# A convolution-plus-MLP kernel on one core: spectra of two chunks at a time, and turns of Z done by transposing transfers

## The chip, the core and the metric

The kernel runs on one core of a Trainium2 chip. TensorE (PE) multiplies matrices into PSUM, and its weight loads (PEld) are shown as a row of their own; VectorE (DVE) and ScalarE (ACT) do the elementwise work and copy PSUM to SBUF; GpSimd (POOL) builds tables; SyncE (SP) issues nearly all transfers, in order, and 16 DMA engines carry them out. The metric is the device time of one execution in microseconds. A profiled execution gives a span (first to last instruction) and a time of its own, which is slightly longer than the span.

## The reference, cut to what matters

```python
# A: a diagonal state-space convolution over L = 2048 positions, D = 512 channels, N = 128 states
P = exp(dt*A[:, :, None] * l)                 # complex, l rounded to bf16
K = einsum("dn,dnl,dn->dl", Cc, P, dt*Bc).real
y = irfft(rfft(pad(u.T)) * rfft(pad(K)))[:, :L]        # causal convolution per channel
h = x + bf16(y).T + u * Dskip,   u = layernorm(x)
# B: an MLP on the result, F = 1376
h2 = h + gelu(layernorm(layernorm(h)) @ w1 + b1) @ w2 + b2
```

The 2048 positions are worked as two blocks of 1024 (block 0 and block 1; in a name of the change "A" and "B"). Block 0 of the output needs block 0 of u and block 0 of K. Block 1 needs u1 with K0 and u0 with K1, and what block 0 carries over.

## The kernel before, in words

One SBUF arena `ar` holds everything; a view is an address in it, and the same address is used by several views in turn. PSUM is four slots of 128x1024 f32. All work is handed to a small planner (`Sched`) as operations with an engine (or a choice of ACT and DVE), a cost, what they read and write, and a rank from the table `RANK`; it places them one after the other and the kernel emits them in that order. Each engine then runs its own list in order, and semaphores follow the true dependences. A "soft" dependence is one of the planner alone: it sets the order of the list and makes no semaphore.

The 512 channels are four chunks of 128 (`CW`, `NCH`). The stages, with the lines of the profile:

- **Setup.** Loads, layernorm statistics of x (L878), and the tables of sines: T, TP1 and TP2 (L605, three of 2048 columns), after int32 codes made on POOL (L584, L1302). T has three parts [cos, sin, cos] per frequency so that a slice of two neighbours gives X or its swapped twin Xs; DVE copies the third part (L582, 128x1024 bf16).
- **aexps** (L960 to L965) fills the powers EA with accumulating matmuls and exponentials, two PSUM slots in turn; L700 and L698 build its 17 scaled identities.
- **austage** (L900) multiplies normalised u by a small block matrix for both blocks and writes it to DRAM (AU_d), to come back with another partition order. This write and read is called a bounce.
- **chain** (L988 to L1014) makes the complex exponentials of K for two halves of the channels: matmuls, a Sin on ACT (L1003), products on DVE (L1013, L1014).
- **kgen** (L1035, L1036) forms K of one chunk with 256 small matmuls (33 columns and 20 output rows each); **kspec** (L1080) does a first transform stage of K for one block and one chunk and writes it to DRAM (AK_d); **kload** (L1096) loads it back and does the second stage, one 128x128 matmul per frequency.
- **xspec0** (L917) does the second stage of u for block 0 and all channels: per frequency two matmuls of 512 columns, [re, im] into X0 and the swapped [im, re] into X0s, 16 PSUM tiles of 1024 columns. **xspec** (L935) does block 1 chunk by chunk, 16 tiles as well, into two buffers XB used in turn.
- **inverse** multiplies spectra on DVE (L1114) and transforms back with TP1 and TP2 (L1123), 128 rows per matmul. Its result Z has to be turned (frequency group and position change places). For chunks 2 and 3 of block 0 (`TURN`) TensorE does it (L1138: 16 transposes, copied out by ACT or DVE). For the six others Z goes to DRAM (Z_d) and comes back in the new order.
- **tail** (L1208, L1213) adds x and the turned Z in PSUM, takes statistics (L1218), runs the short layernorm chain (L593, L598, L582, L584 on 128x4), normalises (L1232, L1234) and transposes with TensorE (L1239); there are four tails, two per block.
- **mlp** (L1257, L1259, L1274, L1276), four of them, and the output.

L536 and L538 are the one helper that copies PSUM to SBUF (`evac`) on ACT or DVE, and L548 the one that issues plain transfers. Products (`PR`), the normalised rows of the tail (`y2s`) and int32 codes share addresses, as do the spectra of block 0, the turned Z and the MLP weights.

Of the kernel before, what the change touches and what calls it, by code (L numbers as in the profile page):

```python
# [1404 lines left out]
```

## Time and profile before

| what | value |
|---|---|
| median of 3 runs | 301.11 us (300.15 to 301.65) |
| profiled execution, own time | 297.31 us |
| its span | 295.5 us |
| granted TensorE clock, mean | 0.971 |
| busy: PE, PEld | 232.2 us, 140.1 us |
| busy: ACT, DVE, POOL | 198.0 us, 185.5 us, 46.0 us |
| DMA moved | 34.15 MB, 43873 of 57191 packets under 512 B |

A busy time is the union of an engine's instructions; the matmuls are pipelined, so the mean duration of one (219 ns for L1123) is far above its share of the busy time. The page also has the span in slices, the chain of work that ended last, groups of instructions by line with what ended the idle time before them, and the transfers with their time from issue to landing.

### The profile page before, as it was taken

The page shows a single profiled execution, that of the slowest core. Times are in us where ns is not written, and L with a number is a line of the kernel's source. Part 1 is how long each engine was busy: PE and PEld are TensorE (multiplying, and loading weights), DVE is VectorE, ACT ScalarE, POOL GpSimd, SP SyncE. Part 2 cuts the span into 40 slices and gives each one's busy share as a digit, 9 for nine tenths or more (in the row PEclk, how much of TensorE's full clock was granted, in tenths as well). Part 3 has the DMA queues.
Part 4 walks back from the last instruction along what each step waited for, and adds up shares of the span by engine and source line. Part 5 has one row for each costly group of instructions (what it writes and reads, how often), then busy time and mean ns, then how long its engine had stood idle before and what let it go on. Part 6 is the DMA issues. An engine that isn't in the chain of part 4 may idle for free.

```text
span 295.5 us, 8030 instructions
## 1 busy us (share of the span) xinstructions
PE 232.2 (79%) x3337; PEld 140.1 (47%) x3360; DVE 185.5 (63%) x392; ACT 198.0 (67%) x257; POOL 46.0 (16%) x213
## 2 busy tenths in 40 slices
PE   6204948788997797499977629799999999898983
PEld 2101313344576546487855226578674334443431
DVE  3999999999986798035736784656850375311021
ACT  5988999999956994157984848685528338832700
POOL 9992102996000000000000000000000000000000
PEclk9999998999999999979999958999999999999999
DMA  7700113799101679997896300656564011002011
GB/s 145 265 0 2 35 41 91 195 231 341 35 4 57 192 167 241 239 235 257 249 219 155 71 1 0 176 141 201 144 159 110 0 46 29 1 18 57 0 35 36
DMA packets 57191, 34.15 MB, mean 116 GB/s; under 512 B 43873, under 2 KB 52034, under 8 KB 57154
## 3 DMA queue, kind: packets, MB, share of 16 engines
q1 hardware_dynamic: 55954, 33.24, 42.3%
q8 instruction: 26, 0.43, 0.6%
q10 hardware_dynamic: 1200, 0.39, 0.5%
q14 instruction: 11, 0.09, 0.1%
HBM read 19.47 MB, written 13.63 MB: 112 GB/s over the span
## 4 chain that ended last, share of the span: by engine, by line
PE 47%; DVE 22%; issue 10%; ACT 9%; DMA 5%; SPq 3%; POOL 2%; DVEq 0%; ACTq 0%; POOLq 0%
PE ps L1274 12%; PE ps L1257 9%; ACT ar L536 6%; PE ps L1123 5%; DVE ar L593 4%; PE ps L1036 3%; SPq L548 3%; PE ps L1035 3%; DVE ar L878 3%; DVE ar L598 3%; DVE ar L538 3%; PE ps L997 2%; PE ps L1080 2%; DMA ar<-AU_d 2%; DVE ar L1218 2%
## 5 line engine op out<-in xcount | busy, mean ns | idle before, releaser
L536 ACT CAST ar<-ps 128x1024 bf16<-128x1024 f32 (+3 forms) x91 | 75.2, 889 | 49.5 <-DVE ar L1218 9.8
L538 DVE CAST ar<-ps 128x1024 bf16<-128x1024 f32 (+2 forms) x33 | 38.8, 1194 | 19.0 <-PE ps L1096 12.8
L1257 PE MATMUL ps<-ar 128*128 128x512 bf16 (+1 forms) x170 | 40.6, 384 | 2.8 <-ACT ar L536 1.4
L1274 PE MATMUL ps<-ar 128*128 128x512 bf16 (+1 forms) x168 | 40.1, 379 | 3.1 <-DVE ar L1276 2.7
L1114 DVE TENSOR_TENSOR ar<-ar 128x1024 bf16<-128x1024 bf16 x48 | 30.1, 688 | 17.1 <-PE ps L1123 14.6
L1259 ACT ACTIVATE ar<-ps,ar 128x512 bf16<-128x512 f32 (+1 forms) x44 | 29.7, 689 | 14.5 <-PE ps L1257 14.1
L1003 ACT ACTIVATE ar<-ps 128x1024 bf16<-128x1024 int16 x36 | 35.5, 1042 | 3.5 <-PE ps L997 3.0
L584 POOL TENSOR_SCALAR ar<-ar 128x128 bf16<-128x128 bf16 (+5 forms) x40 | 30.5, 783 | 15.6 <-DMA ar<-ar 10.4
L1276 DVE TENSOR_TENSOR ar<-ps,ar 128x512 bf16<-128x512 f32 x16 | 11.0, 690 | 32.7 <-PE ps L1274 25.6
L1257 PEld LDWEIGHTS <-ar 128*128 128x128 bf16 (+1 forms) x176 | 17.6, 101 | 22.1 <-issue 4.3
L1274 PEld LDWEIGHTS <-ar 128*128 128x128 bf16 (+1 forms) x176 | 16.7, 97 | 22.8 <-issue 4.9
L1036 PE MATMUL ps<-ar 128*20 128x33 bf16 x512 | 20.0, 248 | 6.6 <-issue 6.6
L1218 DVE BATCH_NORM_STATS2 ar<-ps 128x6 f32<-128x512 f32 x16 | 11.1, 697 | 21.7 <-PE ps L1213 16.7
L1123 PE MATMUL ps<-ar 128*128 128x128 bf16 x384 | 24.1, 219 | 0.6 <-DVE ar L1114 0.3
L997 PE MATMUL ps<-ar 128*32 128x256 f16 x560 | 21.4, 275 | 3.8 <-ACT ar L1003 1.6
L1123 PEld LDWEIGHTS <-ar 128*128 128x128 bf16 x384 | 22.3, 98 | 3.3 <-DVE ar L1114 1.0
L1036 PEld LDWEIGHTS <-ar 128*20 128x20 bf16 x512 | 17.8, 125 | 8.2 <-issue 8.2
L997 PEld LDWEIGHTS <-ar 128*32 128x32 f16 x560 | 13.9, 97 | 12.6 <-issue 12.1
L1035 PE MATMUL ps<-ar 128*20 128x33 bf16 x512 | 19.7, 249 | 0.2
L1014 DVE TENSOR_TENSOR ar<-ar 128x1024 bf16<-128x1024 bf16 x26 | 17.8, 702 | 1.6 <-ACT ar L1003 1.5
L1013 DVE TENSOR_TENSOR ar<-ar 128x1024 bf16<-128x1024 bf16 x26 | 18.1, 709 | 0.9 <-ACT ar L1003 0.8
L1035 PEld LDWEIGHTS <-ar 128*20 128x20 bf16 x512 | 17.5, 124 | 0.5 <-issue 0.2
(92 smaller groups left out, 307.8 us busy)
## 6 DMA issues: line engine op xcount, KB each, us to landing
AU_d<-ar SPq DMA_DIRECT2D x16, 256.0 KB, 4.6
ar<-AU_d SPq DMA_DIRECT2D x8, 512.0 KB, 5.9
AK_d<-ar SPq DMA_DIRECT2D x16, 256.0 KB, 4.2
ar<-AK_d SPq DMA_DIRECT2D x8, 512.0 KB, 5.6
Z_d<-ar SPq DMA_DIRECT2D x12, 256.0 KB, 3.2
ar<-Z_d SPq DMA_DIRECT2D x6, 512.0 KB, 4.6
ar<-in_A_u_dram SPq DMA_DIRECT2D x4, 512.0 KB, 7.1
ar<-in_A_u_dram SPq DMA_DIRECT2D x16, 128.0 KB, 5.4
```

What stands on the lines that cost most here:

```text
L536: act.copy(out_fn(), in_fn())
L538: dve.tensor_copy(out_fn(), in_fn())
L584: en.tensor_scalar(a, b, f(s1), f(s2), op0, op1)
L997: pe.matmul(pst(p)[32 * g:32 * g + 32, 256 * j:256 * j + 256], lhsT=W2[DELTAS.index(d)].ap(), rhs=S2[g].ap()[:, ch0:ch0 + 256], start=Fals ...
L1003: add("ACT", c_act(1024), lambda e, p=p, sc=sc, cs=cs: act.activation(sc[cs].ap().rearrange("p a b -> p (a b)"), pst(p, i16).rearrange("p ...
L1035: pe.matmul(o, lhsT=Ar.ap()[:, :, d], rhs=Br.ap()[:, :, d], start=True, stop=False, tile_position=(0, 32 * g))
L1036: pe.matmul(o, lhsT=Ai.ap()[:, :, d], rhs=Bi.ap()[:, :, d], start=False, stop=True, tile_position=(0, 32 * g))
L1114: add("DVE", c_dve(1024, 2), lambda e, kf=kf, x=x, pr_=pr_, f0=f0: dve.tensor_tensor(pr_.ap(), kf[f0:f0 + 8].ap(), x[f0:f0 + 8].ap(), ALU. ...
L1123: pe.matmul(pst(p)[:, 128 * k:128 * k + 128], lhsT=a, rhs=b_, start=(n == 0), stop=(n == len(jobs) - 1))
L1257: pe.matmul(pst(p)[:fs, 512 * z:512 * z + 512], lhsT=w1s[dc].ap()[:, fc * P:fc * P + fs], rhs=ybuf.ap()[:, dc, :], start=(dc == 0), stop=( ...
L1259: add("ACT", c_act(512, 1), lambda e, p=p, z=z, fc=fc, fs=fs: act.activation(hT.ap()[:fs, fc, :], pst(p)[:fs, 512 * z:512 * z + 512], ACT. ...
L1274: pe.matmul(pst(p)[:, 512 * z:512 * z + 512], lhsT=hT.ap()[:fs, fc, 128 * t:128 * t + 128], rhs=w2s[fc].ap()[:fs], start=(fc == 0), stop=( ...
```

## The change

The parts of a spectrum (real and imaginary) are laid in the free dimension: two neighbouring frequencies share the 128 partitions, 64 each. One stage (`fstage`) now serves u and K. It uses 64-column weights in two column positions of the array, and its output holds each value once, so that the swapped twins X0s and Xs are gone; the product reads X with its two parts reversed. The inverse uses 64-row matmuls in two row positions, into two PSUM banks. K is staged for two chunks at a time (`kgen` still works by chunk): chunks 0 and 1 for both blocks in one bounce, chunks 2 and 3 in one bounce per block. All of block 1's K is staged ahead of the tails, and block 1's u is loaded and transformed in one go into a buffer of its own. Every turn of Z, and the transposes of three of the four tails, are transposing transfers from SBUF to SBUF on SP's queue, 128x2048 bf16 each; only the first tail keeps TensorE transposes. Products, Z, x rows and normalised rows have buffers per block, and the addresses of weights and spectra move with them. aexps takes turns in three PSUM slots and needs 19 scaled identities. The rank table is another one, with two constants of the planner's model.

```diff
-NZ = 3
-NKG = 3
-TURN = (2, 3)
+KB = [[(0, 1)], [(0,), (1,)]]
...
-    AK_d = [[dram.tile([16, P, CW], bf16, name=f"AK_d{b}{c}") for c in range(NCH)] for b in range(2)]
-    Z_d = [[dram.tile([P, 16, CW], bf16, name=f"Z_d{b}{c}") for c in range(NCH)] for b in range(2)]
+    AK_d = [[dram.tile([16, P, 2 * CW * len(bs)], bf16, name=f"AK_d{q}{n}") for n, bs in enumerate(KB[q])] for q in range(2)]
...
-    T = take(bf16, 16, 3, 64)
-    TP1 = take(bf16, 16, P)
-    TP2 = take(bf16, 16, P)
+    T = take(bf16, 16, 2, 64)
+    TP = [take(bf16, 8, P) for _ in range(3)]
...
+    def xspec(b, X, pr, soft=()):
         S.pr = pr
         for q in range(4):
...
+        fstage(X, 4, soft)
+    def fstage(v, nb, soft=()):
+        pr, w = S.pr, 128 * nb
+        nf = 8 // nb
+        for f0 in range(0, 16, nf):
             p = Ps()
             def fn(e, p=p, f0=f0):
+                for k in range(0, nf, 2):
                     for r in range(2):
+                        for h in range(2):
+                            f = f0 + k + h
+                            pe.matmul(pst(p)[64 * h:64 * h + 64, w * (k + r):w * (k + r) + w], lhsT=T.ap()[:, f, r, :], rhs=v.ap()[:, f, :], start=True, stop=True, tile_position=(0, 64 * h))
+            evac(lambda f0=f0: v[f0:f0 + nf].ap().rearrange("p a b -> p (a b)"), lambda p=p: pst(p), 1024, [p], [v[f0:f0 + nf]])
...
+    def kstage(q, ak, D, kf, bs, pr):
+        nb = len(bs)
+        for n, b in enumerate(bs):
+            kspec(b, q, pr + n, ak, nb, n)
+        for cp in range(2):
+            dma("SP", lambda cp=cp: D.rearrange("(k z) p d -> z p k d", z=2)[cp], lambda cp=cp: ak.ap()[:, 8 * cp:8 * cp + 8, :], 524288 * nb, ...)
+        for fh in range(2 * nb):
+            dma("SP", lambda fh=fh, n=n: kf[n * fh:n * fh + n].ap(), ..., 524288, ...)
+        fstage(kf, 2 * nb)
...
+                    def mul(e, kf=kf, X=X, sw=sw, pr_=pr_, f0=f0):
+                        a, b_, o = (q.ap().rearrange("p (a r) d -> p a r d", r=2) for q in (kf[f0:f0 + 8], X[f0:f0 + 8], pr_))
+                        dve.tensor_tensor(o, a, b_[:, :, ::-1, :] if sw else b_, ALU.mult)
...
+                for k in range(4):
+                    for n, (q, w0, w1) in enumerate(jobs):
+                        for r, w in enumerate((w0, w1)):
+                            for h in range(2):
+                                rows = slice(64 * h, 64 * h + 64)
+                                pe.matmul(pst(p)[:, 512 * h + 128 * k:512 * h + 128 * k + 128], lhsT=q.ap()[rows, 2 * k + r, :], rhs=TP[w].ap()[rows, f0 // 2 + k, :], ..., tile_position=(64 * h, 0))
+            evac(lambda f0=f0: zw.ap()[:, :, f0:f0 + 8].rearrange("p q (k h) -> p q k h", h=2), lambda p=p: pst(p).rearrange("p (h k q) -> p q k h", h=2, k=4), 1024, [p], [zw])
+        turn(zt, lambda: zw.ap().rearrange("p (s q) f -> p s (q f)", s=16), zw)
+    def turn(o, i_ap, i):
+        add("SP", 2.2, lambda e: nc.sync.dma_start(o.ap(), i_ap(), transpose=True), r=[i], w=[o], byts=450000)
...
+        if not first:
+            turn(ybuf, lambda: y2s[sb].ap().rearrange("p t (c k) -> p (t c) k", c=4), y2s[sb])
...
-    TS(T, T, 1.0, None, ALU.mult, n=1024, mode=4, oap=lambda: T.ap()[:, :, 2, :], iap=lambda: T.ap()[:, :, 0, :], pr=2.99)
...
-    for c in range(NCH):
-        kgen(c, 5.1 + 4 * c)
-        kspec(0, c, 5.2 + 4 * c)
-        kspec(1, c, 6.2 + 4 * c)
-        kload(0, c, KF0[c], 5.25 + 4 * c)
-        inverse(0, c, [(KF0[c], (XR[c][0], XR[c][1]))], ZT0[c], 2 * c, 5.3 + 4 * c, c in TURN)
+    for q in range(2):
+        for c in (2 * q, 2 * q + 1):
+            kgen(c, 5.1 + 4 * c)
+        for n, bs in enumerate(KB[q]):
+            kstage(q, AKb[q][n], AK_d[q][n], KF[q][n], bs, 9.2 + 8 * q + n)
+        for c in (2 * q, 2 * q + 1):
+            inverse(0, c, [(KFb[0][c], XR[c])], ZT0[c], 10.3 + 8 * q + 0.1 * c)
...
+    xspec(1, XB, 18.8)
     for c in range(NCH):
-        xspec(1, c, XB[c % 2], 50 + 3 * c)
-        kload(1, c, KF1[c % 2], 51 + 3 * c)
-        inverse(1, c, [(KF0[c], XB[c % 2]), (KF1[c % 2], (XR[c][0], XR[c][1]))], ZT1[c], 2 * c, 52 + 3 * c)
+        inverse(1, c, [(KFb[0][c], XBc[c]), (KFb[1][c], XR[c])], ZT1[c], 52 + 3 * c)
```

More of the change, by code (lines that the diff above doesn't have):

```diff
@@ L496 @@
     pos[0] = rest0 + 8192
-    XR = [(VS(X0, c), VS(X0s, c)) for c in range(NCH)]
-    Kg = [take(bf16, NB, 32) for _ in range(NKG)]
-    AK = [take(bf16, 16, CW) for _ in range(2)]
-    PR = [take(bf16, 8, CW) for _ in range(4)]
-    Z = [take(bf16, 8, CW) for _ in range(NZ)]
+    XR = [VS(X0, c) for c in range(NCH)]
+    Kg = [take(bf16, NB, 2, 32) for _ in range(2)]
+    AK0 = take(bf16, 16, 2 * CW).lo
+    XB = take(bf16, 16, 512)
+    hs = [at(BA0 + 26624 + 1024 * n, bf16, 512) for n in range(8)] + [at(E0 + 1024 * n, bf16, 512) for n in range(8)]
+    PR = [[at(lo + 2048 * n, bf16, 8, CW) for n in range(4)] for lo in (rest0, BA0 + 34816)]
+    Z = [[at(lo, bf16, P, 16) for lo in q] for q in ((sc0 + 8192, sc0 + 12288), (BA0 + 8192, Kg[0].lo + 11264))]
     assert pos[0] <= NBYTES, pos[0]
@@ L691 @@
     POOL(1.3, cv_fn, w=[cv, hv], pr=0.2)
-    LD = [LA[a] - (LA[a - 4] if a >= 4 else 0) for a in range(NA)]
+    LD = [LA[a] - (LA[a - 6] if a >= 6 else 0) for a in range(NA)]
     LV = sorted(set(LD), key=LD.index)
@@ L841 @@
     PTS(Jt, Ji, 1.0)
[L842 to L845 removed]
+    skc = ct(i32, 8)
+    POOL(0.2, lambda: gp.iota(skc.ap(), pattern=[[128, 8]], base=16, channel_multiplier=0), w=[skc])
+    sk = ct(f32, 8)
+    PTS(sk, skc, f64, f2s, op0=ALU.add, op1=ALU.add)
     valD = ct(f32, 2, 16)
@@ L949, in aexps @@
     def aexps(pr):
-        ps = [Ps("e", 3), Ps("e", 3)]
+        ps = [Ps("e", 3) for _ in range(3)]
         for n in range(NA // 2):
-            p = ps[n & 1]
+            p = ps[n % 3]
             def fn(e, p=p, n=n):
@@ L1100, with kspec, mm @@
-    npr = [0]
-    def inverse(b, c, pairs, zt, nz, pr, turn=False):
-        S.pr = pr
+            evac(ofn, ifn, NB * n * N, [p], [kg])
+        add("DVE", c_dve(32), lambda e: dve.tensor_tensor(kg.ap()[:, 0, c & 1], kg.ap()[:, 0, c & 1], Dz.ap()[:, c, :], ALU.add), r=[kg, Dz], w=[kg])
+    def kspec(b, q, pr, ak, nb, n):
+        kg = Kg[q]
+        for cp in range(2):
+            S.pr = pr + 0.01 * cp
+            ps = [Ps(), Ps()]
+            first = True
+            for par in (None, 0, 1):
+                vs = [(v, cy) for v, (blk, cp_, par_, cy) in enumerate(VARS) if blk == b and cp_ == cp and par_ == par]
+                if not vs:
+                    continue
+                def mm(e, ps=ps, par=par, vs=vs):
+                    js = [(v, cy, tl) for v, cy in vs for tl in range(4)]
+                    for m, (v, cy, tl) in enumerate(js):
+                        for g in range(4):
+                            rows = slice(32 * g, 32 * g + NA)
+                            k0 = 8 * tl + cy
+                            oo = pst(ps[g // 2])[:, 512 * (g % 2):512 * (g % 2) + 512].rearrange("p (c k i) -> p k c i", c=2, k=8)
+                            r = kg.ap()[rows, k0:k0 + 8] if par is None else kg.ap()[rows, k0 + par:min(k0 + 8, NB):2]
+                            if par is not None:
+                                oo = oo[:, par:8:2]
+                            pe.matmul(oo, lhsT=W[v].ap()[rows, tl, :], rhs=r, start=(m == 0), stop=(m == len(js) - 1), tile_position=(32 * g, 0))
+                add("PE", 4 * len(vs) * (0.22 if par is None else 0.12), mm, r=[kg, W], w=ps, new=ps if first else [])
+                first = False
+            for h in range(2):
+                evac(lambda cp=cp, h=h: ak[8 * cp:8 * cp + 8].ap().rearrange("p k (c b d) -> p b c k d", c=2, b=nb)[:, n, :, :, 64 * h:64 * h + 64].rearrange("p c k (g i) -> p c k g i", g=2),
+                     lambda ps=ps, h=h: pst(ps[h]).rearrange("p (g c k i) -> p c k g i", g=2, c=2, k=8), 1024, [ps[h]], [ak[8 * cp:8 * cp + 8]])
@@ L1105, in inverse @@
+    npr = [0, 0]
+    nzw = [0, 0]
+    def inverse(b, c, pairs, zt, pr):
+        S.pr = pr
+        zw = Z[b][nzw[b] % 2]
+        nzw[b] += 1
         for fh in range(2):
@@ L1107, in inverse @@
             p = Ps()
-            z = Z[(nz + fh) % NZ]
             jobs = []
-            for kf, (X, Xs) in pairs:
-                for x, TPx in ((X, TP1), (Xs, TP2)):
-                    pr_ = PR[npr[0] % 4]
-                    npr[0] += 1
-                    add("DVE", c_dve(1024, 2), lambda e, kf=kf, x=x, pr_=pr_, f0=f0: dve.tensor_tensor(pr_.ap(), kf[f0:f0 + 8].ap(), x[f0:f0 + 8].ap(), ALU.mult), r=[kf[f0:f0 + 8], x[f0:f0 + 8]], w=[pr_])
-                    jobs.append((pr_, TPx))
-            def fn(e, p=p, jobs=jobs, f0=f0):
-                for k in range(8):
-                    for n, (q, TPx) in enumerate(jobs):
-                        a, b_ = TPx[f0 + k].ap(), q.ap()[:, k, :]
-                        if turn:
-                            a, b_ = b_, a
-                        pe.matmul(pst(p)[:, 128 * k:128 * k + 128], lhsT=a, rhs=b_, start=(n == 0), stop=(n == len(jobs) - 1))
@@ L1124, in inverse @@
-            add("PE", 0.5 * len(jobs), fn, r=[q for q, _ in jobs] + [TP1, TP2], w=[p], new=[p])
-            if turn:
-                zw = at(Z[0].lo, bf16, P, 16)
-                for sh in range(2):
-                    evac(lambda f0=f0, sh=sh, zw=zw: zw.ap()[:, 64 * sh:64 * sh + 64, f0:f0 + 8], lambda p=p, sh=sh: pst(p).rearrange("p (f q) -> p q f", f=8)[:, 64 * sh:64 * sh + 64, :], 512, [p], [zw])
-                continue
-            evac(lambda z=z: z.ap().rearrange("p a b -> p (a b)"), lambda p=p: pst(p), 1024, [p], [z])
@@ L1131, in inverse @@
-            dma("SP", lambda z=z, f0=f0: Z_d[b][c][:, f0:f0 + 8, :], lambda z=z: z.ap(), 262144, [z], [("Z", b, c, fh)])
-        if turn:
-            for sh in range(2):
-                p = Ps()
-                def tfn(e, p=p, sh=sh):
-                    for s in range(8):
-                        pe.transpose(pst(p, bf16)[:, 128 * s:128 * s + 128], zw.ap().rearrange("p (s q) f -> p s (q f)", s=16)[:, 8 * sh + s, :], identb.ap())
-                add("PE", 0.5, tfn, r=[zw, identb], w=[p], new=[p])
-                evac(lambda sh=sh: zt[8 * sh:8 * sh + 8].ap().rearrange("p a b -> p (a b)"), lambda p=p: pst(p, bf16)[:, 0:1024], 1024, [p], [zt[8 * sh:8 * sh + 8]])
-            return
@@ L1142, in inverse @@
-        zv = Z_d[b][c].rearrange("(s g r) f d -> (g r f) s d", g=4, r=2) if False else Z_d[b][c].rearrange("(s q) f d -> s (q f) d", q=8).rearrange("s q d -> q s d")
-        dma("SP", lambda: zt.ap(), lambda: zv, 524288, [("Z", b, c, 0), ("Z", b, c, 1)], [zt], k=1.2)
+            for kf, X in pairs:
+                for sw in range(2):
+                    pr_ = PR[b][npr[b] % 4]
+                    npr[b] += 1
+                    def mul(e, kf=kf, X=X, sw=sw, pr_=pr_, f0=f0):
+                        a, b_, o = (q.ap().rearrange("p (a r) d -> p a r d", r=2) for q in (kf[f0:f0 + 8], X[f0:f0 + 8], pr_))
+                        dve.tensor_tensor(o, a, b_[:, :, ::-1, :] if sw else b_, ALU.mult)
+                    add("DVE", c_dve(1024, 2), mul, r=[kf[f0:f0 + 8], X[f0:f0 + 8]], w=[pr_])
+                    jobs.append((pr_, 2 if sw else 0, 2 if sw else 1))
@@ new lines, in fn @@
+            def fn(e, p=p, jobs=jobs, f0=f0):
+                for k in range(4):
+                    for n, (q, w0, w1) in enumerate(jobs):
+                        for r, w in enumerate((w0, w1)):
+                            for h in range(2):
+                                rows = slice(64 * h, 64 * h + 64)
+                                pe.matmul(pst(p)[:, 512 * h + 128 * k:512 * h + 128 * k + 128], lhsT=q.ap()[rows, 2 * k + r, :], rhs=TP[w].ap()[rows, f0 // 2 + k, :], start=(n == 0 and r == 0), stop=(n == len(jobs) - 1 and r == 1), tile_position=(64 * h, 0))
@@ L1200, in tail @@
         nb = nw2[2 * b + sb]
+        first = b == 0 and sb == 0
         for jp in range(2):
@@ L1221, in tail @@
         for jp in range(2):
-            p = Ps()
+            p = Ps() if first else None
             for z in range(2):
```

160 lines of the change are left out of this document (52 added, 108 removed), and 68 rows, old and new, of the table RANK.

## The prediction, made blind

> **What bounds the kernel now.** I read the page first (busy times, chain of waits), then a table of busy time in six stages, then the groups of instructions by shape, then the chain and the timeline inside the stages that the change touches.
>
> ```profile
> PE 232.2 (79%) x3337; PEld 140.1 (47%) x3360; DVE 185.5 (63%) x392; ACT 198.0 (67%) x257; POOL 46.0 (16%) x213
> PE 47%; DVE 22%; issue 10%; ACT 9%; DMA 5%; SPq 3%; POOL 2%; DVEq 0%; ACTq 0%; POOLq 0%
> ```
>
> PE holds half of the chain, but it is an average over stages with different limits. The stage table (columns: stage, length, busy PE, PEld, DVE, ACT, POOL with counts, granted clock, DMA share, GB/s):
>
> ```profile
> 0.00:52.00 52.00, 27.64 (x127) 11.24 (x129) 47.48 (x131) 46.09 (x70) 26.37 (x186) 0.97 0.31 83
> 52.00:113.00 61.00, 50.86 (x1273) 32.26 (x1279) 54.42 (x80) 52.65 (x57) 19.66 (x28) 1.00 0.57 158
> 113.00:160.00 47.00, 37.94 (x1104) 32.88 (x1104) 23.56 (x30) 29.54 (x36) 0.00 (x0) 0.96 0.90 230
> 160.00:177.00 17.00, 8.15 (x71) 4.23 (x61) 12.46 (x48) 9.67 (x14) 0.00 (x0) 0.79 0.23 51
> 177.00:254.00 77.00, 74.29 (x619) 44.26 (x630) 41.91 (x98) 45.73 (x62) 0.00 (x0) 0.98 0.36 97
> 254.00:295.50 41.50, 33.31 (x161) 15.25 (x161) 5.65 (x9) 14.35 (x21) 0.00 (x0) 1.00 0.11 26
> ```
>
> Setup and chains (to 113) belong to DVE and ACT; from 113 to 160 the transfers are busiest (0.90); from 160 to 177 the first two tails leave PE idle for 17 - 8.15 = 8.85 us; from 177 to 254 PE is the bound (74.3 of 77); the end is the last two MLPs. Only PE work taken out of 177 to 254, earlier starts before 177, or work moved into the hole at 160 can show in the time.
>
> **The change, part by part.** These are the groups that it touches (line, engine, shape, count, then busy us and mean ns):
>
> ```profile
> L536 ACT CAST ar<-ps 128x1024 bf16<-128x1024 f32 x61 | 59.2, 1031 | 24.3 <-PE ps L1123 8.0 <-PE ps L1080 5.7 <-PE ps L935 4.2
> L538 DVE CAST ar<-ps 128x1024 bf16<-128x1024 f32 x31 | 37.2, 1219 | 16.5 <-PE ps L1096 12.8 <-PE ps L935 1.5 <-ACT ar L1003 1.0
> L1114 DVE TENSOR_TENSOR ar<-ar 128x1024 bf16<-128x1024 bf16 x48 | 30.1, 688 | 17.1 <-PE ps L1123 14.6 <-PE ps L1239 1.7 <-ACT ar L536 0.8
> L1123 PE MATMUL ps<-ar 128*128 128x128 bf16 x384 | 24.1, 219 | 0.6 <-DVE ar L1114 0.3
> L1080 PE MATMUL ps<-ar 20*128 20x256 bf16 x256 | 10.2, 289 | 0.4 <-ACT ar L536 0.3
> L605 ACT ACTIVATE ar<-ar 128x2048 bf16<-128x2048 int16 x3 | 5.8, 1932 | 0.0
> L700 DVE TENSOR_SCALAR ar<-ar 128x128 f16<-128x128 bf16 x11 | 1.3, 241 | 2.1 <-POOL ar L631 2.1
> L582 DVE TENSOR_SCALAR ar<-ar 128x1024 bf16<-128x1024 bf16 x1 | 0.4, 406 | 0.0
> ```
>
> *Setup.* The third part of T goes (0.41 us of DVE) and one Sin of 2048 columns' worth goes too: three of 1.93 become one of 1.93 and three of 1024 columns, which by the 1.03 us of the ACT copy of that size make 5.0 for 5.8. Two more scaled identities cost 0.24 each. I take -0.5 (from -1.2 to +0.5; GpSimd's half-sized codes are not on the chain).
>
> *Spectra of block 0's u.* Sixteen PSUM tiles become eight; the eight copies saved cost 1.03 on ACT or 1.22 on DVE, shared by both 1.03 x 1.22 / 2.25 = 0.56 each. At 99 to 113 these copies stand among the last chain steps, and both engines are full:
>
> ```profile
> 99.00:113.00 14.00, 11.29 (x219) 6.36 (x208) 12.69 (x14) 12.76 (x14) 0.00 (x0) 1.00 0.76 196
> ```
>
> So 8 x 0.56 = 4.5 is nearly all on the path to the third chunk's kgen: -4 (0 to -4.5).
>
> *K of chunks 2 and 3, and the last bounce before the first tail (113 to 160).* The parts that stand on the chain, and the transfers (KB each, us from issue to landing):
>
> ```profile
> 118.69 1.09 issue
> 122.11 2.77 issue
> 157.86 1.11 PE ps L1138 x16
> 160.19 0.32 PE ps L1208
> AK_d<-ar SPq DMA_DIRECT2D x16, 256.0 KB, 4.2
> ar<-AK_d SPq DMA_DIRECT2D x8, 512.0 KB, 5.6
> Z_d<-ar SPq DMA_DIRECT2D x12, 256.0 KB, 3.2
> ar<-Z_d SPq DMA_DIRECT2D x6, 512.0 KB, 4.6
> ar<-ar SPq DMA_DIRECT2D x16, 32.0 KB, 1.9
> ```
>
> The last bounce of block 0 now carries two chunks: 0.5 MB more written and 0.5 MB more read, 2.2 us each at the 230 GB/s of this stage, +4.4. After it two chunks have to be multiplied and not one, four more products of 0.69, +2.5 with the start of the second overlapped. The turn of the last chunk was 160.19 - 157.86 = 2.3 us on PE; now it is a transfer. No row shows a transposing transfer. Below it can hardly be cheaper than the plain 512 KB read of Z, 4.6 us; above, if it goes 128x128 block by 128x128 block (32 KB each, the size of the restacking pieces), 16 pieces one after the other at 1.9 are 30 us. I take 6, by the row of the same size: +3.7. Against that: the eight copies of block 1's u that PE and ACT did here (half of L935's work) halve or leave, 8 x 0.56 = -4.5; the two issue waits inside kgen come while DMA is full, and since AK is written in rows of 512 B and 1 KB instead of 256 B, I take half of them, -2, and -2 for the writing itself. Sum: 4.4 + 2.5 + 3.7 - 4.5 - 2 - 2 = +2. Bounds: -6 when the larger rows make both bounces as quick as one of before; +10 when block 1's K and u, whose loads are moved on SP's queue from after 160 to before it (4 x 0.5 MB of u alone are 8.7 us at 230 GB/s), stand ahead of the path's transfers.
>
> The wait that the change adds: SP waits for a chunk's second copy of Z before it issues the turn; behind it on SP stand weights, x rows and the next turns, and the tail's matmuls wait for these. The old Z writes waited in the same way.
>
> The Trainium skill has a rule that speaks against these turns: "VectorE: DVE Perf Modes", section The three transpose paths, gives 1309 ns for a 128x128 block by the DMA crossbar against 390 on TensorE. Sixteen in a row are an estimate of 21 us; with the three exposed turns of the first rival below, that page's figure makes the time about 331. Its page "Advanced Engine Details and Errata", section X-Bar Transpose (TRN2), says on the contrary that transposing transfers run as fast as regular ones, which would give the sum as it stands. No row here shows which holds.
>
> *The hole at 160 to 177.* Block 1's spectra and products had to wait there: two XB buffers, and products in the addresses of the normalised rows. With buffers per block and u loaded early PE can do spectra and inverses of block 1 in it. DVE is busy 12.5 of 17, so only some four of the eight product groups fit: -5. Statistics of the second tail no longer stand between the steps of the first one's short chain:
>
> ```profile
> 168.89 0.70 DVE ar L1218
> 170.32 0.60 DVE ar L1218
> 171.00 0.60 DVE ar L1218
> 173.67 0.42 DVE ar L1232
> ```
>
> The three long pieces are 1.9 us ahead of L1232: -2. Together -7 (0, when the planner puts nothing in, to the whole 8.85).
>
> *177 to 254.* Busy time of the three lines that shrink, in this stage alone (L935, L1096, L1239 in this order; PE busy, PEld busy, clock, DMA):
>
> ```profile
> 177.00:254.00 77.00, 4.57 (x64) 3.92 (x64) 0.98 0.36 97
> 177.00:254.00 77.00, 2.11 (x32) 1.87 (x32) 0.98 0.36 97
> 177.00:254.00 77.00, 2.89 (x32) 2.54 (x32) 0.98 0.36 97
> 165.00 0.39 PE L1208 MATMUL ps<-ar 128*128 128x512 bf16 x1
> 165.31 0.41 PE L1213 MATMUL ps<-ar 128*64 128x512 bf16 x2
> 165.65 0.39 PE L1208 MATMUL ps<-ar 128*128 128x512 bf16 x1
> L1274 PE MATMUL ps<-ar 128*128 128x512 bf16 x152 | 37.2, 379 | 3.1 <-DVE ar L1276 2.7
> ```
>
> The second K stage leaves (-2.1), the transposes become transfers (-2.9), and the spectra become 16 pairs of 64-column matmuls of 512. The next rows price a pair: two L1213 matmuls start together and last 0.41 us where one L1208 lasts 0.39, so a pair costs one. The next starts come 0.31 and 0.34 later; matmuls of 512 columns that follow each other with no such change take 37.2 / 152 = 0.24 (last row): about 0.1 us per change between whole and split array. Sixteen pairs at 0.22 to 0.24 are 3.5 to 3.8 for 4.57: -1.1. Eight inverse tiles between MLP matmuls make 16 changes: +1.6. Sum -4.5 (bounds -9.6, all three lines gone, to +1).
>
> ```profile
> 177.00:254.00 77.00, 15.60 (x256) 14.92 (x256) 0.98 0.36 97
> 254.00:295.50 41.50, 1.22 (x16) 1.06 (x16) 1.00 0.11 26
> ```
>
> The inverse itself I cost at nothing: 384 matmuls of 128 rows become 768 of 64 rows, two at a time. What hides the second is the other half of the array. The kspec rows speak for it: 256 matmuls in 20 rows of 289 ns each, four row groups, take only 10.2 us. If the halves ran one after the other, block 1's 15.6 us (first row) would double. The product with reversed parts has the same size and type as L1114, and I leave it at 0.69; kspec with 512 columns streams the same columns.
>
> *254 to the end.* The fourth tail's transposes (last row): -1.2, covered by the third MLP.
>
> **Sum.** -0.5 - 4 + 2 - 7 - 4.5 - 1.2 = -15.2. The profiled execution took 297.31 by its own time, 1.8 more than its span, and 3.8 less than the median of 301.11. 297.3 - 15.2 = 282.1; with the same 3.8, 286 for the median.
>
> **The rivals.**
>
> 1. *Turns are slow, slower than before.* If a turn goes in 16 pieces at the spacing of the restacking issues, it takes 10.1 + 1.9 = 12 us and not 6:
>
> ```profile
> 37.38 10.08 SPq L548 DMA_DIRECT2D ar<-ar  x16
> ```
>
> Two turns in a row stand ahead of the first tail and one ahead of the third: 3 x 6 = 18 more, 304. From about 11 us per turn (15.2 / 3 above 6) the gain is gone. For it: no row shows a transposing transfer. Against: 512 KB moves in 4.6 to 5.6 in the other rows.
>
> 2. *The coarse bounce eats it.* The last bounce at its bad bound (+8 on my +2) and a hole filled by 2 only (+5): 286 + 13 = 299. For: DMA share 0.90 already. Against: 256-byte rows go.
>
> 3. *More than forecast.* The bounces at their good bound (-8) and the hole full with the spectra of 177 to 254 moved into it too (-4): 274. For: PE is the only bound after 160; ACT and DVE together lose 22 copies of 1.03 to 1.22, some 24 us of busy time (8 and 8 for the spectra of u, 6 for the tails). Against: each stage has its own wait.
>
> 4. *Halves of the array don't overlap.* +15.6 in the PE-bound stage: 301.6, and up to 8.5 more for block 0.
>
> **How the numbers follow.** Forecast 0.47, rivals 0.12, 0.17, 0.18 and 0.06. The forecast's own range is 278 to 293. Rivals 2 and 3 lie inside 270 to 303; outside are the far half of 1 and 4 and a still larger gain, under 0.2. A measurement of this kernel can tell about 0.5% (1.5 us) from no change. Faster: 0.47 + 0.18 + 0.6 x 0.17 = 0.75; same: the rest of 2 and half of 4, 0.10; slower: 1 and half of 4, 0.15.
>
> **What would show it.** A turn of 128x2048 landing near 6 us; L1114 still near 690 ns; inverse matmuls, now 768, still near 24 us busy; 22 fewer copies of 1024; PE over 0.7 busy in the stage of the first two tails; the first tail starting within some 5 us of 160; busy PE between tail one and tail three down by 4 to 10 us. A turn above 11 us, inverse matmuls near 48 us, or a first tail after 168 would make it wrong.

## The result, and the profile after

The changed kernel took **291.44 us** (median of four runs, 289.11 to 295.04), the kernel before 300.63 beside it: a ratio of **0.966 (95% interval 0.960 to 0.973)**, 9 us faster. The prediction was 286, 15 us faster, with 278 to 293 as the forecast's own range. So sign and range held and the size did not. That the time fell into the range is luck in part: the sections below show that one step of the sum was wrong by some 20 us, and others by 11 the other way.

An execution more than 1.5% above the fastest one of its kernel counts in the medians here and not in the ratios, and the profile that came with the result is of such a one (295.04 us). So the lines below are those of the same kernel profiled once more, 290.43 us by its own time and 288.6 of span; the kernel before has 297.31 and 295.5.

From the page of the changed kernel: busy times, then transfers.

```profile
PE 229.3 (79%) x3302; PEld 124.5 (43%) x3316; DVE 180.2 (62%) x393; ACT 176.7 (61%) x228; POOL 36.8 (13%) x213
DMA packets 47879, 33.63 MB, mean 116 GB/s; under 512 B 29441, under 2 KB 43746, under 8 KB 47842
```

ACT lost 21 us and DVE 5, yet PE, which holds the end, lost only 2.9. The stage table, in the stages of the prediction:

```profile
0.00:52.00 52.00, 26.71 (x101) 10.71 (x102) 48.94 (x130) 42.97 (x68) 27.24 (x198) 0.97 0.26 70
52.00:113.00 61.00, 51.10 (x1332) 31.69 (x1338) 50.90 (x80) 49.91 (x54) 9.01 (x15) 0.96 0.55 166
113.00:160.00 47.00, 41.81 (x1004) 27.15 (x996) 25.66 (x36) 30.49 (x34) 0.52 (x1) 0.86 0.83 229
160.00:177.00 17.00, 11.74 (x273) 9.53 (x267) 11.05 (x18) 8.82 (x9) 0.00 (x0) 0.90 1.04 211
177.00:254.00 77.00, 71.20 (x494) 33.60 (x503) 38.31 (x125) 37.09 (x55) 0.00 (x0) 0.96 0.28 57
254.00:288.60 34.60, 26.72 (x120) 11.81 (x120) 5.39 (x8) 7.45 (x11) 0.00 (x0) 0.96 0.13 31
```

The stage 160 to 177 looks like a hole that was partly filled, as forecast. It isn't: the first tail, which made that hole, has moved. Its first matmul (L1208 before, L1184 after) came at 160.2 us and now comes at 174.6:

```profile
L1184 PE MATMUL ps<-ar x12: 377/390/608, 174.6 to 232.2; 128*128 128x512 bf16 x12
```

Its next matmuls read the turned Z (L1189), and they wait 2.2 us more for a transposing transfer:

```profile
177.22 0.64 PE L1189 MATMUL ps<-ar 128*64 128x512 bf16 x2 [2.21 <-DMA ar<-ar]
```

So the better cut is at the first tail of each kernel. The kernel before, then the changed one (same columns: length, busy PE, PEld, DVE, ACT, POOL, clock, DMA share, GB/s):

```profile
0.00:160.20 160.20, 116.64 (x2505) 76.48 (x2513) 125.46 (x239) 128.28 (x162) 46.03 (x213) 0.98 0.58 155
160.20:295.50 135.30, 115.55 (x833) 63.64 (x848) 60.02 (x153) 69.75 (x95) 0.00 (x0) 0.96 0.26 69
```

```profile
0.00:174.60 174.60, 130.96 (x2687) 78.99 (x2692) 134.85 (x259) 131.17 (x161) 36.77 (x213) 0.93 0.58 158
174.60:288.60 114.00, 98.33 (x619) 45.51 (x624) 45.39 (x135) 45.56 (x67) 0.00 (x0) 0.96 0.25 52
```

Ahead of the first tail PE's idle time is the same: 160.2 - 116.6 = 43.6 and 174.6 - 131.0 = 43.6. The tail comes 14.4 us later, and PE is busy 14.3 us longer before it (in part because its clock is lower, 0.93 for 0.98). Behind it PE is busy 17.2 us less (115.6 to 98.3) and idles 15.7 and not 19.8. By PE's account the whole difference of the two spans, 6.9 us, is 2.9 of busy time gone and 4.1 of idle time behind the first tail gone. What moved ahead is block 1's work: 576 of the 768 inverse matmuls (256 of block 0 and 320 of block 1, where only block 0's stood ahead before) and all of the spectra (groups by line, split at 174.6; columns length, busy PE, busy PEld, clock, DMA share, GB/s; L1112, then L924):

```profile
0.00:174.60 174.60, 19.58 (x576) 17.43 (x576) 0.93 0.58 158
174.60:288.60 114.00, 7.57 (x196) 6.62 (x192) 0.96 0.25 52
0.00:174.60 174.60, 20.26 (x160) 8.73 (x160) 0.93 0.58 158
```

The groups that answer to those of the prediction, and the turns (us from issue to landing):

```profile
L534 ACT CAST ar<-ps 128x1024 bf16<-128x1024 f32 x59 | 57.2, 1025 | 28.0 <-PE ps L1112 10.0 <-PE ps L1062 7.9 <-PE ps L924 7.1
L536 DVE CAST ar<-ps 128x1024 bf16<-128x1024 f32 x21 | 25.1, 1218 | 17.6 <-PE ps L924 13.6 <-PE ps L1062 4.0
L1102 DVE TENSOR_TENSOR ar<-ar 128x1024 bf16<-128x1024 bf16 x48 | 30.0, 685 | 3.3 <-PE ps L1112 3.2
L1112 PE MATMUL ps<-ar 64*128 64x128 bf16 x768 | 27.1, 228 | 2.9 <-DVE ar L1102 2.0 <-ACT ar L534 0.2
L924 PE MATMUL ps<-ar 128*64 128x512 bf16 x96 | 15.6, 446 | 2.3 <-DMA ar<-AK_d 2.0 <-ACT ar L534 0.2 <-DVE ar L536 0.2
ar<-ar SPq DMA_TRANSPOSE x11, 4.4
AK_d<-ar SPq DMA_DIRECT2D x2, 1024.0 KB, 5.1
ar<-AK_d SPq DMA_DIRECT2D x8, 512.0 KB, 5.7
```

The eighty copies of 1024 in these rows were 92; with the copies of transposes, which have rows of their own, 104 became 82. The products keep their 685 ns; the halves of the array do overlap (27.1 us for 768 matmuls, where 384 whole ones took 24.1); a turn lands after 4.4 us.

### The profile page after: what moved, and what is told of

It reads as the page before. It is cut to its first block, busy times and chain, and to the rows that moved or that the text cites. A ratio compares the mean times of both kernels' runs of the same rounds, so it can differ in the third digit from the quotient of the medians.

```text
span 293.3 us, 7914 instructions
## 1 busy us (share of the span) xinstructions
PE 233.0 (79%) x3316; PEld 123.9 (42%) x3316; DVE 180.8 (62%) x393; ACT 177.1 (60%) x228; POOL 37.6 (13%) x213
## 3 DMA queue, kind: packets, MB, share of 16 engines
q1 hardware_dynamic: 46642, 32.72, 43.6%
## 5 line engine op out<-in xcount | busy, mean ns | idle before, releaser
L534 ACT CAST ar<-ps 128x1024 bf16<-128x1024 f32 (+3 forms) x75 | 66.3, 932 | 54.8 <-PE ps L1189 14.8
L536 DVE CAST ar<-ps 128x1024 bf16<-128x1024 f32 (+3 forms) x29 | 30.7, 1074 | 29.0 <-PE ps L924 9.9
L992 ACT ACTIVATE ar<-ps 128x1024 bf16<-128x1024 int16 x36 | 34.7, 1033 | 4.4 <-PE ps L986 2.9
L1102 DVE TENSOR_TENSOR ar<-ar 128x1024 bf16<-128x1024 bf16 x48 | 30.0, 686 | 2.8 <-PE ps L1112 2.7
L1112 PE MATMUL ps<-ar 64*128 64x128 bf16 x768 | 26.2, 222 | 3.8 <-DVE ar L1102 2.9
L1112 PEld LDWEIGHTS <-ar 64*128 64x128 bf16 x768 | 22.7, 97 | 8.1 <-DVE ar L1102 6.1
L582 POOL TENSOR_SCALAR ar<-ar 128x128 bf16<-128x128 bf16 (+5 forms) x40 | 22.5, 589 | 12.7 <-ACT ar L603 11.7
L1026 PE MATMUL ps<-ar 128*20 128x33 bf16 x512 | 20.1, 248 | 4.3 <-issue 4.3
L1025 PE MATMUL ps<-ar 128*20 128x33 bf16 x512 | 20.2, 249 | 3.9 <-issue 2.9
L924 PE MATMUL ps<-ar 128*64 128x512 bf16 (+1 forms) x160 | 21.2, 399 | 2.6 <-DMA ar<-AK_d 2.3
L1025 PEld LDWEIGHTS <-ar 128*20 128x20 bf16 x512 | 17.3, 124 | 12.7 <-issue 11.4
L739 ACT ACTIVATE ar<-ar 128x512 bf16<-128x512 f32 x32 | 17.2, 615 | 2.6 <-DVE ar L591 2.6
L986 PEld LDWEIGHTS <-ar 128*32 128x32 f16 x560 | 13.8, 98 | 11.0 <-issue 10.7
L1026 PEld LDWEIGHTS <-ar 128*20 128x20 bf16 x512 | 17.8, 126 | 0.0
L1002 DVE TENSOR_TENSOR ar<-ar 128x1024 bf16<-128x1024 bf16 x26 | 17.5, 689 | 0.4
```

Source lines behind the costliest of these rows:

```text
L534: act.copy(out_fn(), in_fn())
L536: dve.tensor_copy(out_fn(), in_fn())
L582: en.tensor_scalar(a, b, f(s1), f(s2), op0, op1)
L986: pe.matmul(pst(p)[32 * g:32 * g + 32, 256 * j:256 * j + 256], lhsT=W2[DELTAS.index(d)].ap(), rhs=S2[g].ap()[:, ch0:ch0 + 256], start=Fals ...
L992: add("ACT", c_act(1024), lambda e, p=p, sc=sc, cs=cs: act.activation(sc[cs].ap().rearrange("p a b -> p (a b)"), pst(p, i16).rearrange("p ...
L1025: pe.matmul(o, lhsT=Ar.ap()[:, :, d], rhs=Br.ap()[:, :, d], start=True, stop=False, tile_position=(0, 32 * g))
```

## The experiments

The theories. **One:** the gain is that block 1's spectral work now stands ahead of the first tail, and the tail's lateness is the price. **Two:** the transposing transfers make that tail late. **Three:** the MLP's weights, loaded at 106 to 121 us, make it late. **Four:** the two-block bounce of K does. **Five:** it is not the structure but the re-searched table of ranks. Each edit is put through the planner anew, which reorders some of the other work too; how many of block 1's inverse matmuls stand ahead of the first tail shows it, and is said where it differs. Ratios are to the kernel before, timed beside.

### The changed kernel again

> The changed kernel unchanged: about 291 us beside about 300.6 for the kernel before, ratio 0.96 to 0.975. A fresh profile is wanted in which the stages can be read without the low clock of 0.946: every theory expects the first tail (L1184) between 174 and 179 us from the span's start, not near 160 as forecast, and TensorE about 0.9 busy from there to the end.

290.3 us (288.17 to 290.89), ratio 0.974 (0.968 to 0.980). It is the yardstick below, and its profile is the one shown above. The same kernel has now come out at 0.966 and at 0.974, and in its other profiled execution the first tail started at 177.3 us. So differences of 0.008 in a ratio, or of some 3 us in the start of that tail, say little.

### Block 1's u after the first tail

```diff
-    xspec(1, XB, 18.8)
+    xspec(1, XB, 18.8, [y2T[0]])   # loads and matmuls are ordered behind the first turned rows
```

> Block 1's rows of u are loaded and transformed only when the first tail's normalised rows exist, instead of ahead of the first tail. Theory 1 (the gain of the change is that block 1's spectral work now stands ahead of the first tail, where the tail waits anyway): the first tail comes some 3 to 6 us earlier, but 7.5 us of products on TensorE and 8 copies of about 1 us move behind it, where TensorE is nine tenths busy: 295 to 301 us, most of the gain gone. Rival (block 1's work ahead of the first tail only makes that tail late): first tail near 168, total 283 to 288 us.

317.0 us, ratio 1.064 (1.056 to 1.071): 27 us slower than the changed kernel. Split at its first tail:

```profile
0.00:159.50 159.50, 112.14 (x2335) 66.55 (x2340) 124.35 (x239) 118.00 (x149) 36.78 (x213) 0.97 0.56 150
159.50:317.30 157.80, 121.96 (x968) 57.87 (x976) 63.77 (x157) 55.01 (x77) 0.00 (x0) 0.88 0.27 61
```

The tail comes at 159.5 us, 15 earlier, near what the prediction had (160.2 - 4.5 + 2 = 157.7). But PE is busy 23.6 us longer behind it, and idles there for 35.8 us and not 15.7. Of the 23.6, 17.8 are block 1's work that was moved (12.9 of inverse, since all 320 of its matmuls from ahead of the tail now stand behind it, and 4.9 of spectra); the granted clock there is 0.88 and not 0.96. PE's longest waits are 8.2 us for a layernorm chain on DVE and 5.2 for a turn: block 1's stages then follow each other with little beside them (the last product runs at 243.4 us, in the changed kernel at 197.2). Theory one holds in its direction, and its price was set too low: I had counted the moved work and not the chain that it makes. So the early bounce of u costs 15 us at the first tail and is worth 44 behind it (157.8 - 114.0). This doesn't show that the early place alone makes the 9 us: with u late, the changed kernel is slower than the one before, which had much of block 1's work behind its tail as well.

### Block 0's turns on TensorE

```diff
+        if b == 0:
+            ...   # per chunk 2 x 8 transposes of 128x128 and 2 copies of 1024, as before for chunks 2 and 3
+            return
         turn(zt, ..., zw)
```

> Block 0's four turns go by 64 TensorE transposes and 8 copies of 1024 elements instead of four transposing transfers. Theory 2 (the transposing transfers, 1.7 to 6.1 us of issue on SyncE and 4.3 to 8.4 us to landing, make the first tail late): first tail 4 to 8 us earlier, total 284 to 288 us. Rival (what is late stands ahead of the turns, in the bounce of K, or the later work fills the time anyway): the first tail moves by under 2 us, and 8 copies of about 1 us on two engines cost 0 to 3 us: 291 to 294 us.

291.3 us, ratio 0.978 (0.972 to 0.984), first tail at 175.5: the rival's numbers. The stretch ahead of the tail suggests why nothing is won (150 to 177 us, this kernel and then the changed one):

```profile
150.00:177.00 27.00, 24.71 (x634) 21.07 (x629) 24.14 (x36) 22.42 (x25) 0.00 (x0) 1.00 0.60 160
```

```profile
150.00:177.00 27.00, 20.80 (x523) 17.33 (x517) 21.05 (x32) 16.57 (x18) 0.00 (x0) 0.94 1.02 201
```

With the turns as transfers the 16 DMA engines are full (1.02); without them they are at 0.60, and PE, DVE and ACT are at 0.92, 0.89 and 0.83 of the stretch. One bound is exchanged for another at the same place. The planner also put 64 fewer of block 1's inverse matmuls ahead of this tail (512 of the 768 stand there, not 576), so the two stretches don't hold quite the same work.

### The weights after K's first return

```diff
-    load_mlp(40, [])
+    load_mlp(40, [("KFR", 0, (0, 1), n) for n in range(4)])
```

> The MLP's weights are loaded only when the first pair's K has come back, out of the stretch 107 to 121 us. Theory 3 (at 107 to 150 us the transfers are the bound, and the weights ahead of the x rows and of K make the first tail late): K's write and load-back 4 to 10 us earlier, first tail at 168 to 173, total 284 to 288 us. Rival (the weights then meet the turns and block 1's rows, and the same bytes stand ahead of the same tail): first tail within 2 us of before the edit, 290 to 294 us.

298.0 us, ratio 0.999 (0.995 to 1.004), first tail at 189.3: 8 us slower. K's first pair came back no sooner (its loads are issued at 131.2 us, 131.6 in the changed kernel), and the weights then stood on SP's queue among the second pair's bounce (columns start, length, queue):

```profile
131.17 1.76 SPq L546 DMA_DIRECT2D ar<-AK_d  x4
132.97 3.75 SPq L546 DMA_DIRECT2D ar<-in_B_w_dram  x6
139.63 0.38 SPq L546 DMA_DIRECT2D AK_d<-ar  x1
140.05 1.69 SPq L546 DMA_DIRECT2D ar<-in_B_w_dram  x2
141.79 4.41 SPq L546 DMA_DIRECT2D AK_d<-ar  x3
146.25 5.23 SPq L546 DMA_DIRECT2D ar<-in_B_w_dram  x7
```

Theory three falls in this form: at 106 to 121 us the weights don't hold up K. Why the tail is later isn't shown. PE waits for none of K's transfers ahead of it, and 704 inverse matmuls stand there and not 576, all but 64 of them.

### Block 0's turns issued twice

```diff
         turn(zt, ..., zw)
+        if b == 0:
+            turn(zt, ..., zw)
```

> Each of block 0's four turns is issued twice, the second one writing the same values again. Theory 2 (a turn's time stands on the path to the first tail): four more issues of 1.7 to 6.1 us on SyncE and landings of 4.3 to 8.4 us put the first tail 8 to 20 us later, 297 to 305 us. Rival (the turns lie beside other work, as replacing them by TensorE transposes suggested, 291.3 beside 290.3): the first tail under 4 us later, 290 to 295 us.

313.1 us, ratio 1.052 (1.042 to 1.062): 23 us slower than the changed kernel, more than theory two had. The first tail comes 12.5 us later, at 187.1, and the transfers are full all the way to it:

```profile
150.00:187.10 37.10, 27.02 (x659) 22.26 (x653) 26.00 (x40) 16.69 (x18) 0.00 (x0) 0.91 1.04 199
187.10:310.10 123.00, 98.07 (x498) 42.23 (x496) 37.69 (x124) 46.55 (x68) 0.00 (x0) 0.93 0.24 47
```

The 12.5 us are not the turns' alone. The planner put 128 more of block 1's inverse matmuls ahead of this tail (704 for 576); PE is busy 138.8 us before it and not 131.0, and idles 48.3 and not 43.6. So 7.8 us are a longer busy time, and 4.7 are idle time. Behind the tail PE idles 9 us more than in the changed kernel (24.9 for 15.7), with 6.2 us in one wait of the first tail for a turn and 4.4 in one of an MLP matmul.

The pages give the price of a turn better. With block 0's four turns the queue's packets took 43.8% of 288.6 us of all 16 engines, without them 38.4% of 290.8, a difference of 14.7 us or 3.7 us of the whole 16 for a turn; with four more they took 45.1% of 310.1, which is 13.5 us more or 3.4 for a turn. So each turn takes 3.4 to 3.7 us of what is full in this stretch. That taking them off gained nothing because PE, DVE and ACT are then nearly full is argued from the rows above and not tested.

### The first pair's bounce per block

```diff
-KB = [[(0, 1)], [(0,), (1,)]]
+KB = [[(0,), (1,)], [(0,), (1,)]]
...   # the views of the first pair's K follow
```

> The first pair's K goes through its bounce per block, as the second pair's does, so that block 0's half can come back before block 1's is made. Theory 4 (both blocks in one bounce delay block 0's products, which begin at 143.7 us in the changed kernel and began near 113 us in the one before): first product 3 to 8 us earlier, first tail 3 to 6 us earlier, total 286 to 289 us. Rival (block 1's work has to be done ahead of the long dense end either way, so block 0's start decides nothing): 290 to 294 us, with two more transfers and smaller rows.

297.3 us, ratio 0.997 (0.992 to 1.002), 7 us slower. Block 0's first product comes at 137.3 us and not 143.7, as theory four has it, but the first tail at 183.4 and not 174.6. An earlier start of block 0 didn't bring its tail forward; the theory falls in this form. Ahead of that tail PE idles 50.6 us and not 43.6, and it waits 11.6 us for K's loads, 6.3 in one go, where the changed kernel waits 4.2. The edit isn't clean, since 640 inverse matmuls stand there and not 576.

### All tails' rows on TensorE

```diff
-        first = b == 0 and sb == 0
+        first = True
```

> All four tails turn their normalised rows by TensorE transposes with 2 copies of 1024 elements each, in place of the transposing transfers of the last three. Expected if that part of the change was worth 3 to 5 us of TensorE, as the prediction has it (48 transposes, a mode change each, in a stage where TensorE is nine tenths busy): 293 to 296 us. Expected if it was worth nothing, since the transposes fit into gaps: 289 to 292 us.

292.0 us, ratio 0.974 (0.963 to 0.985): not told from the changed kernel. The prediction's -2.9 - 1.2 for these transposes had them on the path. In the profile PE is busy 2.3 us longer behind the first tail (100.6 for 98.3) and idles 12.0 us there and not 15.7: they fit into gaps.

### The kernel before, with six turns as transfers

```diff
+        if turn == "dma":
+            add("SP", 2.2, lambda e: nc.sync.dma_start(zt.ap(), ..., transpose=True), r=[zw], w=[zt], byts=450000)
+            return
...
-        inverse(0, c, ..., c in TURN)
+        inverse(0, c, ..., True if c in TURN else "dma")
...
-        inverse(1, c, ..., 52 + 3 * c)
+        inverse(1, c, ..., 52 + 3 * c, "dma")
```

> The kernel before, with its six turns of Z that went through memory made by transposing transfers; all else as before. If the new turns alone carry a good part of the gain (2.1 MB less written and read, 44% fewer short packets): 294 to 297 us, ratio under 0.99. If the turns by themselves are worth nothing and the order of block 1's work carries the gain: ratio 0.995 to 1.01; and slower, 303 to 308 us, if a turn of 4 to 8 us on SyncE holds up what is queued behind it.

302.9 us, ratio 1.020 (1.009 to 1.031): no gain, and 2% over the kernel before. From the first tail (162.3) to the end it takes 137.7 us, about as long as in the kernel before (135.3), against 114.0 in the changed one. In this form the turns alone don't help. Not all else is as before, though: the six chunks also take the form that chunks 2 and 3 had, with one buffer for Z and each copy of 1024 elements made in two halves, and PE is busy 238.5 us and not 232.2. The premise of the expectation was off too: 3.15 MB less is moved (31.00 for 34.15), but the packets under 512 B are as many as before (43777 for 43873).

### Both kernels with an empty table of ranks

```diff
-RANK = {"0S": 103, ..., "74S": 247}
+RANK = {}
```

> The changed kernel with an empty table of ranks, so that the planner orders the work by its own costs and the written due times alone. To be held beside the kernel before with its table emptied likewise. If the change's own structure carries the gain (fewer copies, two chunks at a time, block 1's work ahead of the first tail): this one is 3 to 4% under that one, as the pair with tables is (0.966 and 0.974). Theory 5 (the re-searched table carries it): the two come out within 1% of each other, both some per cent above their versions with tables, 300 to 315 us.

> The kernel before with an empty table of ranks. If the table is worth a few per cent to it: 303 to 315 us. If the structure carries the gain, the changed kernel without its table lies 3 to 4% under this one; by theory 5 within 1% of it.

Changed kernel 301.1 us, ratio 0.992 (0.987 to 0.997); kernel before 325.8, ratio 1.090 (1.082 to 1.097). Without tables the change makes 0.992 / 1.090 = 0.910, and by the medians 301.1 / 325.8 = 0.924. Theory five falls: the structure, with the due times written into it, brings more when neither order has been searched, 8 to 9%, and the searched table of before had won back most of it (8%; that of the changed kernel is worth 2 to 3%). The split at the first tail (the kernel before without its table, then the changed one without) has nearly the same difference behind the tail as the pair with tables, 137.7 against 118.2, while the tail itself comes no later:

```profile
0.00:185.30 185.30, 127.33 (x2523) 82.18 (x2528) 128.94 (x238) 133.62 (x167) 53.08 (x213) 0.93 0.53 138
185.30:323.00 137.70, 117.77 (x822) 63.61 (x834) 60.19 (x155) 65.25 (x91) 0.00 (x0) 0.95 0.23 62
```

```profile
0.00:181.50 181.50, 130.48 (x2561) 77.42 (x2565) 135.72 (x252) 127.45 (x159) 47.14 (x213) 0.92 0.54 148
181.50:299.70 118.20, 101.16 (x746) 47.46 (x752) 47.55 (x138) 49.84 (x74) 0.00 (x0) 1.00 0.28 58
```

### Block 1's x rows after the first tail

```diff
-    load_x(1, 65)
+    load_x(1, 65, [y2T[0]])
```

> In the changed kernel the eight loads of block 1's x rows (1 MB, issued at 163 to 179 us among the turns, while the transfers are full) are held back until the first tail's turned rows exist; the engines' order ahead of that tail stays as it is. If these loads make the turns and so the first tail late: the first tail at 170 to 173 instead of 174.6 us, total 286 to 289 us. Rival (the first tail stands behind the products and inverses on VectorE and TensorE, not behind the transfers): first tail within 1 us, total 289 to 292 us.

292.4 us, ratio 0.977 (0.970 to 0.984), first tail at 178.8 in its profile: no gain. As many inverse matmuls (576) stand ahead of the tail as in the changed kernel, so this is the cleanest of these edits. Of the 4.2 us by which this tail is later, 3.2 were lost before the held-back loads have their place: the loads of the second pair's K are issued at 147.85 us, in the changed kernel at 144.67. The transfers stay full at 160 to 177 us without these loads (1.02): the turns of block 1 move up into the room. SP's queue of that kernel:

```profile
165.64 1.05 SPq L546 DMA_DIRECT2D ar<-AK_d  x2
...
167.07 21.45 SPq L1118 DMA_TRANSPOSE ar<-ar  x4
188.61 5.58 SPq L546 DMA_DIRECT2D ar<-in_A_u_dram  x8
```

### Two of block 0's turns each way

```diff
+        if b == 0 and c >= 2:   # chunks 2, 3 on TensorE, chunks 0, 1 as transfers
+            ...
+            return
         turn(zt, ..., zw)
```

> In the changed kernel, of block 0's four turns the last two go by TensorE transposes (4 copies of 1024 elements more) and the first two stay transposing transfers. With all four as transfers the stretch ahead of the first tail has its transfers full (share 1.04 at 160 to 177 us) and TensorE at 11.7 us of 17; with all four on TensorE the transfers fall to 0.55 and TensorE rises to 15.4 of 17, and the first tail came at the same 175 us both times. If each bound alone holds the tail there, half of each frees some 7 us of transfers and gives half of the engines' work back: first tail at 171 to 173, total 285 to 288 us, ratio 0.955 to 0.97. Rival (what holds the first tail is block 1's products and inverses ahead of it, whichever way the turns go): first tail within 1.5 us of 175, total 289 to 292 us, ratio 0.97 to 0.98.

289.2 us, ratio 0.967 (0.961 to 0.973), first tail at 173.8 us. That lies between the two expectations, and the changed kernel itself came out at 0.966 and 0.974. So whether half of each is better stays open. Here too 512 inverse matmuls stand ahead of the tail and not 576. At 160 to 177 us its transfers are at 1.06 and PE at 15.4 of 17, so both bounds are met at once.

## Why the prediction was right and where it was wrong

**Setup and block 0's spectra, -4.5: right in its direction.** The last chain product starts at 104.9 us and not at 112.0, 7.1 earlier. Not all of that is saved: 160 of K's first-stage matmuls (L1080) ran ahead of that product before, and none (L1062) does now. The count of copies was right, 22 of 1024 fewer. The scaled identities, put at 0.24 each, were not: 15 of them take 4.8 us of DVE.

**"K of chunks 2 and 3, and the last bounce before the first tail (113 to 160)", +2: the step that failed.** From the last chain product to the first tail it was 48.2 us before and is 69.7 now, +21.5, beyond the step's bad bound of +10. These are the two stretches, before and after:

```profile
112.00:160.20 48.20, 38.14 (x1105) 32.98 (x1105) 24.56 (x32) 29.71 (x37) 0.00 (x0) 0.96 0.91 229
104.90:174.60 69.70, 60.13 (x1500) 41.13 (x1488) 37.59 (x55) 43.30 (x47) 0.52 (x1) 0.88 0.86 223
```

PE idles as long as before (48.2 - 38.1 = 10.1, 69.7 - 60.1 = 9.6) and is busy 22.0 us longer. By lines, the inverse takes 11.2 more (L1112 19.7, L1123 8.5), the second transform stage 5.6 more (L924 16.3; L1096 and L935 10.7), and K's making and first stage 8.2 more (36.8 for 28.6), a part of which stood ahead of the last chain product before; the transposes and the tail's first matmul go, -2.7. By the granted clocks, 38.1 x 0.96 = 36.6 and 60.1 x 0.88 = 52.9, an estimate, some 16 of the 22 are work and the rest is the lower clock.

The parts that I had priced are not the reason. The 1 MB writes land after 5.1 us and the loads after 5.7, the turn after 4.4 (I took 6). The four 512 KB writes of the second pair are late, 8.3 us where the 256 KB ones took 4.2, but PE's waits for K's loads in this stretch only rise from 1.9 to 4.2 us, and its waits for issue within kgen fall (over the whole run from 6.8 to 4.9). What I left out is block 1's work on PE, DVE and ACT. I had allowed for its loads on SP's queue, but had its spectra, products and inverses run in the hole behind the tail's start. The engines work in order, and the planner put this work ahead of the tail. Holding back block 1's u alone brings the tail to 159.5 us; from the last chain product (105.7 there) that is 53.8 us, +5.6, so that without this work the step holds within its bounds.

**The hole -7, 177 to 254 -4.5, the end -1.2: direction right, size wrong in the other direction.** Together -12.7; from the first tail to the end it is 135.3 - 114.0 = 21.3 less. The hole was not filled from behind but emptied from ahead: PE's busy time in this part fell by 17.2 us and rose by 14.3 ahead of the tail, so that 2.9 are gone, and the idle time fell by 4.1, no more. The -2 for a shorter chain of statistics doesn't show: from the first tail's first matmul to its transposes it is 15.3 us (174.6 to 189.9), where it was 14.0 (160.1 to 174.1), and 2.2 of that is the wait for a turn. So the sum came out as -7.1 + 21.5 - 21.3 = -6.9 in the profiles, where -15.2 was forecast.

**The work that went.** The rows on PE that shrink do shrink, to 20.3 us of spectra and K (L924) from 26.6, and 1.4 of transposes from 6.0. PE's total fell by only 2.9. A part of the rest is the clock: the 96 spectrum matmuls of 512 columns have a mean of 446 ns, where the whole-array ones of that width (L917) had 379. At 113 to 160 us the granted clock is 0.86 for 0.96. Three windows of 3 us in that stage show it, and a row of PE's timeline the wait for K in the first of them:

```profile
135.00:138.00 3.00, 1.69 (x8) 0.54 (x8) 1.70 (x2) 0.58 (x1) 0.00 (x0) 0.67 1.00 296
138.00:141.00 3.00, 3.00 (x22) 1.15 (x22) 0.00 (x0) 1.93 (x3) 0.00 (x0) 0.50 1.01 350
141.00:144.00 3.00, 2.84 (x24) 1.22 (x24) 2.59 (x3) 2.16 (x3) 0.52 (x1) 0.70 0.75 226
```

```profile
136.31 1.92 PE L924 MATMUL ps<-ar 128*64 128x512 bf16 x8 [2.01 <-DMA ar<-AK_d]
```

That the wait causes the low clock is only argued; no run here tested it.

**The rivals.** Slow turns: no, 4.4 us, where plain loads of 512 KB land after 4.9 to 6.3. The Trainium skill's "Advanced Engine Details and Errata", section X-Bar Transpose (TRN2), has transposing transfers as fast as regular ones, and this trace agrees as to the landing; as to the time that they take of the DMA engines it doesn't (see the last section). The estimate of 21 us from the Trainium skill's "VectorE: DVE Perf Modes", section The three transpose paths, isn't borne out by the 4.4 us. Halves one after the other: no, 27.1 us for the 24.1 of before. The coarse bounce that eats the gain: more than its price was paid at the first tail (rival two had +8 there), but by another mechanism, and it was given back behind. More than forecast: the 274 would have needed block 1's work to be hidden, and it is only moved.

**The signs named beforehand.** The turn, the products, the copies, PE above 0.7 in the first tails' stage (14.2 of 18 at 177 to 195) came as said. Two did not. PE's busy time between tail one and tail three was to fall by 4 to 10 us and fell by 32.6 (59.2 to 26.6), which is the moved work again. The first tail was to start near 160, and one after 168 had been named as what would make the forecast wrong; it made the reasons wrong and not the time.

## What to carry to other kernels

When work is to fill a hole on an engine that runs in order, ask on which side of the instruction that makes the hole it will be issued: ahead of it, it delays the very thing that waits; behind it, it has to be ready by then, with all its loads. Cut both profiles at the same event, not at the same time, and compare busy and idle time on each side: here that turned a hole that seemed filled into work that was moved. And where an edit takes a load off one resource, look at what else is nearly full in the same stretch before counting the saving.
